# Three one-element clears on GpSimd between the last scatters and the end of the program

## The chip, the cores and the metric

The kernel runs on one core of one Trainium2 chip. The metric is the device time of one execution in microseconds, the median of several runs. The engines are named as in the profile: PE (TensorE matmul), PEld (TensorE weight load), DVE (VectorE), ACT (ScalarE), POOL (GpSimd) and SP (SyncE). A name with a q behind it (POOLq, SPq) is the engine's instruction sequencer, which loads registers, branches, waits on semaphores and drains.

## The reference

Three stages follow one another: windowed attention with a few global keys (2 batches, 8 heads, 768 positions, head size 64), a dense gated feed-forward layer on the 1536 tokens that result, and a mixture of experts in which each token goes to its two best of eight experts. The last stage is the one that matters here:

```python
for e in range(E):
    for k in range(2):
        mask = top2[:, k] == e
        if not mask.any():
            continue
        h = np.maximum(x[mask] @ w1[e], 0.0)
        out[mask] += top2_w[mask, k, None] * (h @ w2[e])
```

The output is 1536 x 512 in float32.

## The kernel before

**The stages.** Attention and the dense layer are interleaved over tiles of 128 tokens. The router then gives every token a slot with each of its two experts, and writes token number and weight to a table in DRAM. The experts run as nine units, numbered 0 to 8. Units 0 and 1 share the expert that leads early, each later unit has one expert of its own with a capacity that falls from 480 to 368 tokens. A unit gathers its tokens' rows, runs two matrix products over eight blocks of the hidden size (`up` at L1041, `down` at L1058 or L1081), and then adds its weighted result to the output.

**How a unit adds to the output.** The output lies in DRAM and is cleared early. For each of its tiles of up to 128 tokens a unit gathers the rows that stand there (`old`, L1018) into a tile `y`, DVE adds the weighted result to `y` (L1110), and `store` writes `y` back by an indirect DMA that POOL issues (L1114). Here an indirect DMA from `y` to the output is called a scatter. Unit 8 is the last. It has 368 slots, so three tiles of 128, 128 and 112 rows, and three scatters. `store` is called for them in the last two lines of `Unit.run`:

```python
            for s, m in self.tiles:
                store(s, m)
```

**What stands behind the scatters.** After the last unit every engine loads a flag (`values_load`, L1302) that says whether an expert had more tokens than its capacity, and branches (L1303) over a slow general path that these inputs don't need. Then the context that builds the program is left (L1382), and it closes the program by itself: SP waits for the semaphore of every DMA and engine, every engine drains and reports to POOL, POOL gives the word to go on, clears a range of semaphores, and there is a second such round. None of that is written in the kernel.

**What sets the order.** Each engine works through its own list of instructions in order. Waits between engines, and between a DMA and an engine, are put in by the framework from what each instruction reads and writes: an instruction that overwrites a tile waits for the semaphore of a DMA that still reads the tile. The scatters' semaphores are called DMASW in the listings of the order.

Of the kernel before, what the change touches and what calls it, by code (L numbers as in the profile page):

```python
# [107 lines left out]
def fused(ctx: ExitStack, tc: tile.TileContext, q, k, v, n_global, n_local, w_gate, w_val, w_out,  # L108
          rms_g, w_router, w_noise, noise, w1, w2, out):
    nc = tc.nc  # L110
# [13 lines left out]
    E, _, F2 = w1.shape  # L124
# [99 lines left out]
    def follow(a, b):  # L224
        tc.add_manual_dep(a, b.name, mybir.DependencyInfo(mybir.DependencyClass.NoSync, mybir.DependencyReason.DATA),
                          reason="order")
# [716 lines left out]
    class Unit:  # L943
# [78 lines left out]
        def run(self, side):  # L1022
            n, cap, gh, gl = self.n, self.cap, self.gh, self.gl
            ending = n == E and len(self.tiles) < 4

            def cuts(s):

                return (slice(0, DM // 2), slice(DM // 2, DM)) if ending and s + 1 == len(self.tiles) else (slice(0, DM),)
# [72 lines left out]
            down(FB2 - 1, prev)  # L1101
            mf = self.me.bitcast(F32)
            done = []

            def store(s, m, turned=None):
                if n > 1:
                    y = self.ys.pop(s)
                    for x, cols in enumerate(cuts(s)):
                        got = acc[s + x][:m, cols] if turned is None else turned[:m, cols]
                        nc.vector.scalar_tensor_tensor(y[:m, cols], got, mf[:m, s, 1:2], y[:m, cols], op0=ALU.mult, op1=ALU.add)  # L1110
                else:
                    y = sb.tile([P, DM], F32, name=f"y{n}_{s}", tag="acc", bufs=NACC)
                    nc.vector.tensor_scalar(y[:m], acc[s][:m], mf[:m, s, 1:2], None, op0=ALU.mult)
                st = nc.gpsimd.indirect_dma_start(  # L1114
                    out=out, out_offset=bass.IndirectOffsetOnAxis(ap=self.me[:m, s, 0:1], axis=0), in_=y[:m],
                    in_offset=None, bounds_check=NT - 1, oob_is_err=False)
                for o in done:
                    tc.declare_no_dep(st.ins, o, reason="a token has one slot per expert")
                done.append(st.ins)
            if wide:  # L1120
                nt = len(self.tiles)
                hs = [pools["b"].tile([P, 2, 2, DC, P], U16, name=f"oT{n}_{x}", tag="raw", bufs=NRAW["b"]) for x in range(2)]
                e, m = self.tiles[-1]
                if m < P:
                    nc.gpsimd.memset(hs[e // 2][:, e % 2].rearrange("p t c q -> p (t c) q")[:, :, m:], 0)
                for c in range(DC):
                    for x in range(2):
                        w = min(2 * P, cap - 2 * x * P)
                        src = acc[c][:, 2 * x * P:2 * x * P + w].bitcast(U16)
                        if w % P and w > P:  # L1130
                            pieces = [(0, 1, P), (1, 1, w - P)]
                        else:
                            pieces = [(0, -(-w // P), min(w, P))]
                        for s0, k, q in pieces:
                            o = hs[x][:, s0:s0 + k, :, c, :q].rearrange("p s t q -> p t s q")
                            i = src[:, 2 * s0 * P:2 * s0 * P + 2 * k * q].rearrange("p (s q t) -> p t s q", t=2, q=q)
                            if c % 2:
                                nc.vector.tensor_copy(o, i)
                            else:
                                nc.scalar.activation(o, i, AF.Copy)  # L1140

                def back(s, m, words, act):
                    pt = sb.tile([P, 512], F32, name=f"pb{n}_{s}", tag="wc", bufs=2)
                    cp = nc.scalar.activation(pt[:m].bitcast(U16).rearrange("p (c q t) -> p t c q", t=2, c=DC),
                                              words[:m].rearrange("p (t c) q -> p t c q", t=2), AF.Copy)
                    follow(cp.ins, act)
                    store(s, m, pt)
                for s, m in self.tiles:
                    if s % 2 == 0:
                        words = sb.tile([P, 2, 2 * DC, P], U16, name=f"ob{n}_{s}", tag="words", bufs=2)  # L1150
                    nc.sync.dma_start_transpose(words[:, s % 2], hs[s // 2][:, s % 2].rearrange("p t c q -> p (t c q)"))
                    tail.append(partial(back, s, m, words[:, s % 2]))
                return
            for s, m in self.tiles:
                store(s, m)

    units = [Unit(0, 0, 0, 0, EARLY), Unit(1, 0, 0, EARLY // P, CAP - EARLY)]

# [3 lines left out]
    n = 0  # L1162
# [224 lines left out]
```

## Time and profile before

| what | us |
|---|---|
| median of 3 runs | 763.89 |
| lowest and highest run | 762.65 and 764.69 |
| the profiled execution, its time | 762.32 |
| the profiled execution, span from first to last instruction | 760.5 |
| PE busy in it | 735.9 |
| POOL busy in it | 318.8 |

The profiled execution's span is 1.8 us shorter than its time; this lies around the program and holds nothing of the kernel. Its time is 1.6 us below the median of the three runs, and these three lie within 2.0 us. PE works for 97% of the span, and the rest of the span is mostly its two ends.

### The profile page before, as it was taken

Reading aid. Unit: us, or ns where it says so; the run is one execution under the profiler, and the core shown is the slowest. Engines: PE = TensorE matmul, PEld = TensorE weight load, DVE = VectorE, ACT = ScalarE, POOL = GpSimd, SP = SyncE. Lnnn points to the kernel's source line nnn. Section 1 sums busy time; section 2 is a strip of 40 time slices with the busy share of each in tenths; the row PEclk is TensorE's granted clock in tenths of the full one; section 3 lists DMA queues with packets and bytes.
Section 4 is the critical chain, followed back from the end, with each engine's and each line's share of the span. In section 5 each row is a group of like instructions: output and inputs, shape, how many; then the busy total and the mean of one; then the engine's idle time right before and its main releaser. Section 6 shows DMA issues by size and latency. Waiting matters only on the chain.

```text
span 760.5 us, 13550 instructions
## 1 busy us (share of the span) xinstructions
PE 735.9 (97%) x4763; PEld 666.6 (88%) x4763; DVE 485.8 (64%) x1134; ACT 410.2 (54%) x878; POOL 318.8 (42%) x350
## 2 busy tenths in 40 slices
PE   9999989999999999999999999999999999999993
PEld 6788989889988888889999989888999999999993
DVE  5998899885497888334535568844555646665641
ACT  5777778675454443114332456536676757776630
POOL 3348853421476566001543144562234345353411
PEclk9999999999999999999999999999999999999997
DMA  8454457533243840002234511989396979898611
GB/s 199 126 166 126 119 135 152 97 85 70 89 135 111 250 137 1 1 6 106 56 57 91 188 29 49 310 240 281 88 264 186 281 175 285 206 323 169 212 41 37
DMA packets 183159, 107.98 MB, mean 142 GB/s; under 512 B 114193, under 2 KB 165393, under 8 KB 183088
## 3 DMA queue, kind: packets, MB, share of 16 engines
q1 hardware_dynamic: 174240, 84.61, 43.0%
q0 software_dynamic: 7120, 19.32, 7.8%
q10 hardware_dynamic: 1728, 3.15, 1.3%
q8 instruction: 39, 0.64, 0.4%
q14 instruction: 32, 0.26, 0.1%
HBM read 75.23 MB, written 16.49 MB: 121 GB/s over the span
## 4 chain that ended last, share of the span: by engine, by line
PE 79%; DVE 7%; DMA 5%; issue 4%; ACT 2%; POOL 1%; SPq 0%; POOLq 0%; ACTq 0%; DVEq 0%
PE pz L1041 17%; PE pz L705 14%; PE acc L732 12%; PE ac L1081 11%; PE pg L705 5%; PE pv L705 5%; PE ac L1058 5%; PE ps L432 3%; PE po L500 1%; DMA ph<-h 1%; PE lg L816 1%; DMA rv<-in_moe_w_val_dram 1%; PE pt L384 1%; PE po L496 1%; DMA y<-out_dram,ic 1%
## 5 line engine op out<-in xcount | busy, mean ns | idle before, releaser
L1041 PE MATMUL pz<-gh,sa 128*128 128x256 f32 (+7 forms) x576 | 154.0, 335 | 2.0 <-POOL sa L686 1.3
L1041 PEld LDWEIGHTS pz<-gh,sa 128*128 128x128 f32 x576 | 103.6, 188 | 7.3 <-POOL sa L686 1.8
L1041 PE MATMUL pz<-gl,sa 128*128 128x256 f32 (+7 forms) x288 | 96.4, 335 | 0.0
L732 PE MATMUL acc<-wo,dh 128*128 128x512 f32 x288 | 88.8, 399 | 0.7 <-ACT dh L718 0.5
L1081 PE MATMUL ac<-zh,sb 128*128 128x480 f32 (+4 forms) x320 | 84.7, 357 | 0.0
L1048 ACT ACTIVATE zh<-pz 128x256 fp32r<-128x256 f32 (+7 forms) x72 | 35.2, 488 | 80.5 <-PE pz L1041 80.5
L1049 DVE SCALAR_TENSOR_TENSOR zl<-pz,zh 128x256 fp32r<-128x256 f32 (+7 forms) x72 | 39.7, 552 | 58.3 <-ACT zh L1048 58.0
L705 PE MATMUL pz<-xTh,wg 128*128 128x256 f32 x352 | 73.9, 286 | 1.3 <-ACT wg L653 1.3
L705 PE MATMUL pz<-xTh,wv 128*128 128x256 f32 x352 | 73.6, 287 | 0.0
L1114 POOL DMA_INDIRECT out_dram<-y,me x30 | 34.2, 1141 | 72.6 <-DVE y L1110 68.7
L1081 PEld LDWEIGHTS ac<-zh,sb 128*128 128x128 f32 x320 | 59.6, 188 | 3.2
L705 PEld LDWEIGHTS pz<-xTh,wg 128*128 128x128 f32 x352 | 58.3, 190 | 3.8 <-ACT wg L653 1.5
L719 POOL TENSOR_TENSOR dl<-u,dh 128x256 fp32r<-128x256 f32 (+1 forms) x38 | 36.9, 972 | 56.6 <-ACT dh L718 31.9
L686 DVE TENSOR_TENSOR sb<-wab,sb 128x512 fp32r<-128x512 f32 x67 | 47.4, 707 | 19.7 <-ACT sb L682 16.8
L686 DVE TENSOR_TENSOR sa<-wab,sa 128x512 fp32r<-128x512 f32 x60 | 44.6, 745 | 23.6 <-ACT sa L682 23.1
L682 ACT ACTIVATE sa<-wab 128x512 fp32r<-128x512 f32 x72 | 44.9, 625 | 27.4 <-PE ac L1081 14.0
L732 PEld LDWEIGHTS acc<-wo,dh 128*128 128x128 f32 x288 | 51.2, 189 | 9.3 <-ACT dh L718 0.7
L705 PEld LDWEIGHTS pz<-xTh,wv 128*128 128x128 f32 x352 | 57.9, 190 | 0.3
L1041 PEld LDWEIGHTS pz<-gl,sa 128*128 128x128 f32 x288 | 54.1, 188 | 2.6 <-DVE gl L1013 0.3
L732 PE MATMUL acc<-wo,dl 128*128 128x512 f32 x144 | 53.5, 397 | 0.0
L1081 PE MATMUL ac<-zl,sb 128*128 128x480 f32 (+4 forms) x160 | 52.4, 358 | 0.0
L1058 PE MATMUL ac<-sb,zh 128*128 128x512 f32 (+1 forms) x176 | 50.6, 375 | 0.0
(255 smaller groups left out, 1841.8 us busy)
## 6 DMA issues: line engine op xcount, KB each, us to landing
wab<-in_moe_w_dram SPq DMA_DIRECT2D x128, 256.0 KB, 6.3
rg<-in_moe_w_gate_dram SPq DMA_DIRECT2D x12, 512.0 KB, 4.5
rv<-in_moe_w_val_dram SPq DMA_DIRECT2D x12, 512.0 KB, 3.6
ro<-in_moe_w_out_dram SPq DMA_DIRECT2D x12, 512.0 KB, 3.6
vn<-in_v_dram SPq DMA_DIRECT2D x12, 256.0 KB, 3.8
out_dram<-zero SPq DMA_DIRECT2D x1, 3072.0 KB, 14.0
x2d<-x ACTq DMA_DIRECT2D x12, 256.0 KB, 5.0
x2p<-hw SPq DMA_DIRECT2D x12, 256.0 KB, 4.6
```

What stands on the lines that cost most here:

```text
L432: seq(nc.tensor.matmul(o, qT[a, h], kT[c][sl, h // 2, C0:], start=(n == 0), stop=(n == len(prods) - 1)))
L682: cp = nc.scalar.activation(wp[:, 0], src, AF.Copy)
L686: sub = (nc.gpsimd if pool else nc.vector).tensor_sub(wp[:, 1], src, wp[:, 0].bitcast(F32))
L705: mm = nc.tensor.matmul(pz, a[:, cs], x[:, tt:tt + nt, c, :], start=(n == 0), stop=(n == 3 * DC - 1))
L719: (nc.gpsimd if ci < len(CHUNKS) - 1 else nc.vector).tensor_sub(dl, u, dh.bitcast(F32))
L732: nc.tensor.matmul(acc[t], a[:, tt], w, start=(f == CHUNKS[ci][0] and n == 0), stop=(end and n == 2))
L1041: mm = nc.tensor.matmul(pz[:, :cap], a[:, cs], x[:, c, :cap], start=(k == 0), stop=(k == 3 * DC - 1))
L1048: self.act = nc.scalar.activation(dh[:, :cap], pz[:, :cap], AF.Relu).ins
L1049: nc.vector.scalar_tensor_tensor(dl[:, :cap], pz[:, :cap], 0.0, dh[:, :cap].bitcast(F32), op0=ALU.max, op1=ALU.subtract)
L1058: mm = nc.tensor.matmul(o, a[:, s * P:s * P + m], w[:, cuts(s)[x]], start=(f == 0 and k == 0), stop=(f == FB2 - 1 and k == 2)).ins
L1081: nc.tensor.matmul(acc[c][:, :cap], w[:, c * P:(c + 1) * P], a[:, :cap], start=(f == 0 and k == 0), stop=(f == FB2 - 1 and k == 2))
L1114: st = nc.gpsimd.indirect_dma_start(out=out, out_offset=bass.IndirectOffsetOnAxis(ap=self.me[:m, s, 0:1], axis=0), in_=y[:m], in_offset=No ...
```

## The change

`Unit.run` keeps the `y` tiles that it stores. In unit 8 (n == E, and E is 8) POOL overwrites the first element of each of the three tiles with zero, after the three scatters have been issued. Each tile is still being read by its scatter, so each clear waits for the semaphore of its scatter. Nothing reads the tiles afterwards, and the output is not touched.

```diff
             down(FB2 - 1, prev)
             mf = self.me.bitcast(F32)
             done = []
+            sent = []
...
                 done.append(st.ins)
+                sent.append(y)
...
             for s, m in self.tiles:
                 store(s, m)
+            if n == E:
+                for y in sent:
+                    nc.gpsimd.memset(y[:1, :1], 0.0)
```

The instructions move at one place, the end of POOL's list. This is that place before: the three gathers of the old rows, the three scatters (`out_dram<-y`), the load of the flag and the branch. DMASW0 to DMASW7 are semaphores of POOL's DMAs, and `DVE` in brackets is a wait for VectorE.

```order
L1018 DMA y_0_8791<-out_dram,ic_8313 128x512 [waits DMASW7_49,DMASW6_49,DMASW5_49]
L1018 DMA y_1_8828<-out_dram,ic_8313 128x512
L1018 DMA y_2_8865<-out_dram,ic_8313 112x512
L1114 DMA out_dram<-y_0_8791,me_8184 1536x512 [waits DMASW1_49,DMASW2_49,DMASW0_49,DVE_49]
L1114 DMA out_dram<-y_1_8828,me_8184 1536x512 [waits DVE_49]
L1114 DMA out_dram<-y_2_8865,me_8184 1536x512 [waits DVE_49]
L1302 TENSOR_LOAD flag [waits DVE_49]
L1303 COMPARE_AND_BRANCH
```

And this is the same place with the change (lines are later by one to five).

```order
L1115 DMA out_dram<-y_0_8791,me_8184 1536x512 [waits DMASW1_49,DMASW2_49,DMASW0_49,DVE_49]
L1115 DMA out_dram<-y_1_8828,me_8184 1536x512 [waits DVE_49]
L1115 DMA out_dram<-y_2_8865,me_8184 1536x512 [waits DVE_49]
L1160 MEMSET y_0_8791 1x1 [waits DMASW3_49]
L1160 MEMSET y_1_8828 1x1 [waits DMASW4_49]
L1160 MEMSET y_2_8865 1x1 [waits DMASW5_49]
L1307 TENSOR_LOAD flag [waits DVE_49]
L1308 COMPARE_AND_BRANCH
```

Three clears stand between the last scatter and the load of the flag, each with a wait for one scatter's semaphore. Nothing moved ahead of them, and the other engines' lists are the same but for line numbers.

## Rows read from the trace of the kernel before

**Rows 1.** Busy time of each engine by stretch, at the end of the program.
```profile
core 0: us, PE busy (x) PEld busy (x) DVE busy (x) ACT busy (x) POOL busy (x), PEclk, DMA share, GB/s
700.00:720.00 20.00, 20.00 (x103) 18.13 (x102) 11.25 (x19) 12.49 (x21) 7.85 (x9) 1.00 0.73 235
740.00:749.00 9.00, 8.00 (x47) 7.04 (x46) 4.80 (x8) 1.92 (x4) 1.72 (x2) 1.00 0.06 23
749.00:751.00 2.00, 0.00 (x0) 0.00 (x0) 0.00 (x0) 0.00 (x0) 1.25 (x2) 1.00 0.47 172
751.00:753.00 2.00, 0.00 (x0) 0.00 (x0) 0.00 (x0) 0.00 (x0) 0.00 (x0) 0.55 0.25 78
753.00:755.00 2.00, 0.00 (x0) 0.00 (x0) 0.00 (x0) 0.00 (x0) 0.00 (x0) 0.50 0.00 0
755.00:760.00 5.00, 0.00 (x0) 0.00 (x0) 0.00 (x0) 0.00 (x0) 0.00 (x0) 0.50 0.00 0
```

**Rows 2.** The chain that ended last, its last four pieces: start us, us, what.
```profile
748.29 1.00 POOL out_dram L1114
749.29 0.08 issue
749.37 0.05 POOLq L1303
749.42 0.13 issue
749.55 1.00 POOLq L1382
```

**Rows 3.** POOL's sequencer in the closing lines: ns min/median/max, first and last start us.
```profile
L1382 POOLq EVENT_SEMAPHORE  x4: 17/17/17, 759.7 to 760.4; - x4
L1382 POOLq DRAIN  x3: 46/113/10069, 749.6 to 760.2; - x3
```

**Rows 4.** The other engines' sequencers in the closing lines, 749 to 760 us.
```profile
L1382 DVEq DRAIN  x2: 10/14/17, 749.0 to 759.9; - x2
L1382 PEldq DRAIN  x2: 8/8/8, 749.2 to 760.0; - x2
```

**Rows 5.** The same for ACT, over the whole span.
```profile
L1382 ACTq DRAIN  x2: 8/8/8, 745.0 to 759.9; - x2
```

**Rows 6.** The same for SP alone, 749 to 754 us.
```profile
L1382 SPq EVENT_SEMAPHORE  x12: 27/28/28, 752.5 to 753.7; - x12
L1382 SPq DRAIN  x2: 7/10/13, 753.8 to 753.8; - x2
```

**Rows 7.** SP's waits from 745 us on: us in total, times, longest.
```profile
SPq L1382 <- PEq L1382: 6.5, 2, 6.0
```

**Rows 8.** POOL's instructions in time at the end: start us, us.
```profile
746.97 1.01 POOL L1114 DMA_INDIRECT out_dram<-y,me  x1 [20.28 <-DVE y L1110]
748.29 1.00 POOL L1114 DMA_INDIRECT out_dram<-y,me  x1 [0.30 <-issue]
749.59 0.96 POOL L1114 DMA_INDIRECT out_dram<-y,me  x1 [0.30 <-issue]
```

**Rows 9.** The last scatter alone (line L1114, from 749.5 us): us to landing.
```profile
DMA to landing us min/median/max: 3.5/3.5/3.5
```

**Rows 10.** Line L1114 from 746 us on, POOL's sequencer ahead of the scatters.
```profile
L1114 POOLq MOVE  x2: 29/29/29, 746.7 to 747.4; - x2
```

**Rows 11.** Line L1110 from 745 us on, DVE's sums that the scatters wait for.
```profile
L1110 DVE SCALAR_TENSOR_TENSOR y<-ac,me,y x4: 484/618/752, 745.9 to 748.0; 128x512 f32<-128x512 f32 x2, 112x256 f32<-112x256 f32 x2
```

**Rows 12.** The load of the flag, line L1302, by engine.
```profile
L1302 SPq TENSOR_LOAD <-flag x1: 268/268/268, 488.4 to 488.4; - x1
...
L1302 POOLq TENSOR_LOAD <-flag x1: 723/723/723, 748.6 to 748.6; - x1
```

**Rows 13.** The smallest clears that POOL makes, line L286.
```profile
L286 POOL MEMSET capv<- x7: 91/91/91, 2.9 to 3.1; 128x1 f32 x7
```

**Rows 14.** POOL's drain at the program's start, line L1368.
```profile
L1368 POOLq DRAIN  x1: 173/173/173, 0.4 to 0.4; - x1
```

**Rows 15.** POOL at an earlier scatter and the instruction behind it.
```profile
718.80 0.97 POOL L1114 DMA_INDIRECT out_dram<-y,me  x1 [0.30 <-DVE zl L1049]
719.79 1.31 POOL L686 TENSOR_TENSOR sa<-wab,sa 128x512 fp32r<-128x512 f32 x1
```

**Rows 16.** All DMAs that POOL issues, by line: count, us to landing.
```profile
out_dram<-y,me POOLq DMA_INDIRECT x30, 4.3
y<-out_dram,ic POOLq DMA_INDIRECT x26, 6.6
...
metad<-meta,si POOLq DMA_INDIRECT x24, 6.5
xg<-x2p,ic POOLq DMA_INDIRECT x22, 5.5
...
xg<-x2d,ic POOLq DMA_INDIRECT x8, 6.6
```

## The prediction, made before the changed kernel ran

> **What bounds the kernel now.** I read the busy times by stretch first, then the end of the chain, then the closing lines engine by engine. The first view shows that PE is the bound almost to the end: it is busy for all of 700 to 720 us, and for 8.00 of the 9.00 us up to 749 us. From 749 us on no matrix, vector or scalar instruction runs, and yet the span goes on to 760.5 us; from 753 us on the DMA engines move nothing either (share 0.00, 0 GB/s) [rows 1]. The change touches only these last 11 us, so only they need to be understood.
>
> The chain ends on POOL: a scatter, the branch, and then a closing instruction that begins at 749.55 us [rows 2]. The chain prints a length of 1.00 us for it; the rows of that line give the true one. It is a DRAIN of 10,069 ns [rows 3], so it ends at 749.55 + 10.07 = 759.62 us, and 0.9 us remain to the end of the span. All others are there long before: the drains of ACT, DVE and PE begin at 745.0, 749.0 and 749.2 us [rows 4, 5], SP passes its twelve waits from 752.5 to 753.7 us and its drain at 753.8 us [rows 6], and then waits 6.0 us [rows 7] (the view names PE's sequencer as the one waited for, but that one was done at 749.2 us, so it is POOL). **POOL's drain alone sets the end**, and it outlasts SP by 5.8 us.
>
> What does the drain wait for? The last scatter is issued from 749.59 to 750.55 us [rows 8] and lands 3.5 us after its start [rows 9], at 753.1 us. SP's waits, which include it, let go at that time, so the landing is real. The drain goes on for 6.5 us more, with nothing in flight and no engine at work. So it does not simply wait for landings. Whether those 6.5 us are work that any first drain has to do, or a price of having begun while scatters were in flight, is the question on which the sign hangs.
>
> **The change, part by part.** The three clears are the nearest to the 128x1 clears of 91 ns [rows 13]; together below 0.3 us, and the first two run while the third still waits. Their waits are the change. Queued behind them on POOL are the load of the flag, the branch, the drain and POOL's word to the closing round, for which all four other engines wait.
>
> Does a clear that waits hold up POOL's sequencer, or does the sequencer go on and drain early? DVE's four sums start from 745.9 to 748.0 us, 750 ns each for the first two [rows 11], so two end at 746.7 and 747.4 us. POOL's sequencer steps from one scatter to the next at 746.7 and 747.4 us [rows 10]: one step when each sum is done. It is held by the wait of the instruction ahead of it. I take that for the clears too.
>
> Then the working is this. The third clear is let go at 753.1 us. The flag's load began at 748.6 us, took 0.72 us [rows 12], and the drain began at 749.55 us [rows 2], so 0.95 us from load to drain. With some 0.05 us for the step, the drain begins at 753.1 + 0.05 + 0.95 = 754.1 us, **4.55 us later** than now.
>
> How long is it then? Two bounds from the same row. All 10.07 us move with it: the span ends 4.6 us later. Or the first 1.00 us of it, up to 750.55 us, was only the wait for the third scatter to be issued [rows 8], which is over by then: 9.07 us remain, it ends at 754.1 + 9.07 = 763.2 us, and the span ends 763.2 - 759.6 = 3.6, say 3.5 us later. I take 3.5, because the overlap with the issue stands in the rows. A cheaper load of the flag (SP's took 0.27 us, not 0.72 [rows 12]) takes off 0.45: 3.1. If the sequencer is not held by the clears, the drain still has to see the third clear done, at about 753.2 us, and then takes its 9.07 us: 762.3 us, 2.6 later. So the likeliest case is +3.5 us between +2.6 and +4.6.
>
> The Trainium skill (Perfetto Trace Analysis, Sequencer-only Instruction) says that the profile's window for a drain begins when its semaphores are satisfied and shows execution alone. By that all 10.07 us would be execution, and the sum +4.6; by the row of the scatter that runs inside the window it is +3.5. No run shown here tells the two apart.
>
> Why is work that moves likelier than a price that goes away? First, the 6.5 us in which nothing is left to wait for. Second, POOL's own instructions are not held by scatters in flight: at 719.79 us a vector operation starts 0.02 us after a scatter's issue ended [rows 15], though scatters take 4.3 us to land [rows 16]. Third, a size that would fit: POOL issued 30 + 26 + 24 + 22 + 8 = 110 DMAs in the program [rows 16], and 9.07 us over 110 is 82 ns each. A drain that goes through all DMAs since the last drain would look like this, and nearly all of these had landed long before. That is an estimate from one division, not a thing seen. POOL's other drains, of 173 ns at the start [rows 14] and 113 and 46 ns at the end [rows 3], have no DMA between them and the drain before, and fit both readings.
>
> Sum: profiled execution 762.32 + 3.5 = 765.8 us. That execution lies 1.6 us under the median of the runs, so against the median it is 763.89 + 3.5 = 767.4 us. Nothing else of the program moves.
>
> **The rivals.** *Faster: the long drain is the price of starting with scatters in flight.* Then a drain that begins at 754.1 us costs what POOL's others do, 0.05 to 0.17 us, POOL gives the word at 754.2 us, just behind SP at 753.8, and the span ends at 754.2 + 0.9 = 755.1 us: 5.4 us less, 758.5 against the median. For it: the only long drain is the only one with DMAs in flight. Against it: the 6.5 us without anything in flight. It decides from the point where the drain after the change lasts under 10.07 - 4.55 = 5.5 us. Chance 0.14. The Trainium skill (VectorE: DVE Perf Modes, The DRAIN you can't avoid) has a rule for it: drains of a program's beginning and end are about 12 ns on all five engines, which would put the end at 755.0 us, 5.5 less. The trace agrees on four engines (7 to 17 ns) and not on POOL.
>
> *No change: the drain's end hangs on something fixed earlier*, such as 9.07 us after the last scatter's issue, however late the drain begins. Since 754.1 us is still ahead of 759.62, all of the new wait would then lie under the old one: 763.9 us. For it: the row can't tell a duration from a deadline. Against: POOL shows no instruction in those 9 us [rows 1]. This is also the case in which the clears do not do what they are for. Chance 0.08.
>
> *The likeliest, later by 2.6 to 4.6 us*: 763.89 + 3.5 = 767.4, and with the runs' own spread 765.2 to 769.3. Chance 0.78.
>
> **How the numbers follow.** A measurement of this kernel can tell about 0.3% from no change, 2.3 us. The likeliest case lies beyond that with all of its bounds, by little at +2.6; I put 0.02 of it within. Faster 0.14, same 0.08 + 0.02 = 0.10, slower 0.76. The range leaves out the faster case and the outer edges; it begins at the low end of the runs of before (762.6, no change) and ends at the highest run plus 4.6 and a little, 769.6.
>
> **What would show it.** In the new profile POOL has three clears, the last at about 753.1 us. If I am right POOL's first closing drain begins near 754.1 us and lasts 9.1 to 10.1 us, and the span is 764 to 765 us. A drain below 0.2 us and a span of 755 us show the faster rival. A drain that ends at 759.6 us shows the deadline. A drain that begins at 749.6 us as before shows that the clears hold nothing. The prediction is wrong in its cause if the drain's length after the last landing depends on what was in flight when it began.

## The result, and the profile after

| | median us | lowest to highest | runs |
|---|---|---|---|
| before | 766.51 | 760.23 to 769.46 | 16 |
| with the three clears | 770.26 | 766.15 to 773.97 | 16 |

The ratio is 1.0051 with a 95% interval of 1.0026 to 1.0076: the change makes the kernel slower by 0.5%, some 3.9 us. The direction and the size against before are as predicted (+3.5 us, 0.46%). The predicted time was not: 770.26 us lies above the range's upper end of 769.6, because before itself came out at 766.51 us over 16 runs, 2.6 us above the three runs that the prediction started from. Those three are the first of the 16.

POOL's closing lines answer to [rows 3]: count, then ns min/median/max, then first and last start in us.

```profile
L1387 POOLq EVENT_SEMAPHORE  x4: 17/17/17, 765.0 to 765.7; - x4
L1387 POOLq DRAIN  x3: 46/107/9057, 755.9 to 765.5; - x3
```

The first closing drain begins at 755.9 us and lasts 9,057 ns. Before, it lasted 10,069 ns, of which the first 1.0 us ran beside the issue of the last scatter; 9.07 us were left then, and 9.06 us it is now, with everything landed before it began (the third clear, which waits for the last landing, runs at 755.11 us, as the next rows show). The drain was not shortened by the wait. It was only started later.

POOL's instructions in time, which answer to [rows 8]: start us, us, and what the engine waited for.

```profile
748.25 1.01 POOL L1115 DMA_INDIRECT out_dram<-y,me  x1 [20.28 <-DVE y L1111]
749.57 1.00 POOL L1115 DMA_INDIRECT out_dram<-y,me  x1 [0.30 <-issue]
750.88 0.96 POOL L1115 DMA_INDIRECT out_dram<-y,me  x1 [0.30 <-issue]
751.80 0.09 POOL L1160 MEMSET y<- 1x1 f32 x1
754.57 0.09 POOL L1160 MEMSET y<- 1x1 f32 x1 [2.69 <-DMA out_dram<-y,me]
755.11 0.09 POOL L1160 MEMSET y<- 1x1 f32 x1 [0.45 <-DMA out_dram<-y,me]
```

The first clear costs no wait, since its scatter has landed by the time the third has been issued. The second and third wait for their scatters, and the third runs at 755.11 us, 4.2 us after its scatter's start. The load of the flag stands behind it, as answers to [rows 12]:

```profile
L1307 POOLq TENSOR_LOAD <-flag x1: 510/510/510, 755.1 to 755.1; - x1
```

Before, it began at 748.6 us, ahead of the last scatter [rows 12]. Now it begins when the third clear is let go, so the waiting clear does hold POOL's sequencer, as [rows 10, 11] had suggested.

The stretches, which answer to [rows 1] (busy us and instructions of each engine, granted clock, DMA share, GB/s):

```profile
752.00:755.00 3.00, 0.00 (x0) 0.00 (x0) 0.00 (x0) 0.00 (x0) 0.09 (x1) 0.63 0.19 57
755.00:757.00 2.00, 0.00 (x0) 0.00 (x0) 0.00 (x0) 0.00 (x0) 0.09 (x1) 0.50 0.00 0
757.00:765.00 8.00, 0.00 (x0) 0.00 (x0) 0.00 (x0) 0.00 (x0) 0.00 (x0) 0.50 0.00 0
```

From 757 to 765 us no engine runs and nothing moves; only POOL's sequencer is in its drain. SP has passed its own waits by 755.9 us and now waits 9.2 us for POOL (its view of waits again names PE's sequencer), where it waited 6.0 us before [rows 7]:

```profile
L1387 SPq DRAIN  x2: 7/10/13, 755.9 to 755.9; - x2
...
SPq L1387 <- PEq L1387: 9.7, 2, 9.2
```

### The profile page after: what moved, and what is told of

It is laid out like the page before. It is cut to its first block, busy times and chain, and to the rows that moved or that the text cites. A ratio compares the mean times of both kernels' runs of the same rounds, so it can differ in the third digit from the quotient of the medians.

```text
span 765.8 us, 13553 instructions
## 1 busy us (share of the span) xinstructions
PE 734.6 (96%) x4763; PEld 665.3 (87%) x4763; DVE 486.5 (64%) x1134; ACT 409.6 (53%) x878; POOL 319.5 (42%) x353
## 4 chain that ended last, share of the span: by engine, by line
PE 76%; DVE 6%; DMA 5%; issue 5%; ACT 4%; POOL 1%; SPq 1%; another core or an unknown queue 1%; POOLq 0%; ACTq 0%; DVEq 0%
PE pz L1041 16%; PE pz L705 14%; PE acc L732 12%; PE ac L1081 10%; PE pg L705 5%; PE pv L705 5%; PE ac L1058 5%; PE ps L432 3%; DMA ph<-h 1%; PE po L500 1%; DMA wab<-in_moe_w_dram 1%; PE lg L816 1%; PE pt L384 1%; PE po L496 1%; DMA out_dram<-y,me 1%
## 5 line engine op out<-in xcount | busy, mean ns | idle before, releaser
L686 DVE TENSOR_TENSOR sb<-wab,sb 128x512 fp32r<-128x512 f32 x67 | 47.6, 711 | 21.7 <-ACT sb L682 16.4
L686 DVE TENSOR_TENSOR sa<-wab,sa 128x512 fp32r<-128x512 f32 x60 | 45.1, 753 | 23.3 <-ACT sa L682 16.8
```

The source lines that it names most:

```text
L686: sub = (nc.gpsimd if pool else nc.vector).tensor_sub(wp[:, 1], src, wp[:, 0].bitcast(F32))
```

## The experiments

**How they are compared.** The start of the last scatter moves from one profiled execution to the next even where the kernels do not differ ahead of it: 749.59 us before [rows 8], 750.88 us with the three clears, 748.58 and 749.36 us with one. In the kernels below that do differ ahead of it, it lies between 745.39 and 753.56 us. So the table at the end of this section takes the time from the last scatter's start to the end of the span. A ratio is to runs of the kernel before in the same group as the experiment's. The two kernels with a drain in unit 8 ran 6 times each, the two with one clear 12 times. The three with further DMAs and the one with a drain in unit 5 ran once each, so of these only the trace is read.

**A drain of POOL's own ahead of the scatters.** The question is whether the closing drain's 9.06 us belong to the DMAs that POOL has issued. If so, a drain in the 20 us in which POOL has nothing to do before the last scatters [rows 8] takes them off the end. On top of before, without clears:

```diff
...
                 if n > 1 and 4 <= f < 4 + len(self.tiles):
                     self.old(f - 4)
+                    if n == E and f == 3 + len(self.tiles):
+                        state["drain"] = nc.gpsimd.drain().ins
+                        follow(state["drain"], self.last_old)
...
+                if n == E:
+                    follow(st.ins, state["drain"])
```

`self.last_old` is the last gather of the unit's old rows, kept in a line that is left out here. `follow(a, b)` puts a behind b in the program's order, without a wait.

> The kernel before, without clears, and with a drain of POOL's own between the last gathers of unit 8 and its three scatters, where POOL has nothing to do for 20 us. Theory (a drain goes through all DMAs that POOL issued since its last drain, 82 ns each): this drain takes 107 x 82 ns = 8.8 us, hidden, and the closing drain has three DMAs left, so it ends with the landing of the last scatter; SP's twelve waits then end the program, and the span is 5.8 us shorter than before (0.8% faster). Rival (a drain behind any DMA of POOL's costs 9.06 us, however many there are): the closing drain still ends 9.07 us after the last scatter's issue, no change.

Measured: ratio 0.9911 (0.9876 to 0.9945), 754.64 us median against 761.26. The new drain's row, the last gather and the next scatter, then POOL's closing lines, POOL's last scatter with its time to landing, and SP's closing drains:

```profile
L1099 POOLq DRAIN  x1: 12502/12502/12502, 720.9 to 720.9; - x1
...
723.14 1.45 POOL L1018 DMA_INDIRECT y<-out_dram,ic  x1 [0.30 <-issue]
744.87 1.01 POOL L1117 DMA_INDIRECT out_dram<-y,me  x1 [20.28 <-DVE y L1113]
...
L1387 POOLq DRAIN  x3: 46/113/3877, 747.4 to 752.5; - x3
...
747.49 0.96 POOL L1117 DMA_INDIRECT out_dram<-y,me  x1 [0.30 <-issue]
DMA to landing us min/median/max: 3.7/3.7/3.7
...
L1387 SPq DRAIN  x3: 7/7/13, 751.9 to 752.2; - x3
```

The drain in the middle took 12.5 us, of which the first 3.7 us waited for two more gathers to be issued (the last from 723.14 us for 1.45), so 8.8 us as expected, and nothing waits for it: the next scatter starts at 744.87 us and waits for DVE as before. The closing drain now ends at 747.4 + 3.9 = 751.3 us, just behind the last landing (751.2 us) and before SP's drains at 751.9, and SP's waits for the landings end the program. From the last scatter's start it takes 5.3 us to the end of the span, where it took 10.9: 5.6 us less, as against 5.8 expected. The rival, a fixed price, falls.

**The same drain, with the clears.**

> The same drain, and the three clears too. Theory: the closing drain begins 0.8 to 1.1 us after the last landing and takes 3 x 82 ns, 0.25 to 0.35 us; about 5.2 us faster than before, and 0.6 us slower than with the drain alone. Rival (9.06 us whatever the count): the closing drain takes 9.06 us after the landing, 3.5 us slower than before.

Measured: ratio 0.9908 (0.9874 to 0.9942). POOL's closing lines and its last scatter:

```profile
L1392 POOLq DRAIN  x3: 46/107/294, 749.7 to 750.6; - x3
...
745.39 0.96 POOL L1118 DMA_INDIRECT out_dram<-y,me  x1 [0.30 <-issue]
```

With three DMAs behind the last drain, and all landed, the closing drain takes 294 ns. The end comes 5.4 us after the last scatter's start, against 5.3 without the clears: once the long drain is gone, the clears cost about nothing, and gain nothing. The 0.6 us expected between the two is not there: POOL's drain ends at 750.0 us and SP's at 749.8 us, so with the clears too the end comes little after SP's waits.

**More DMAs, with many rows and with few.** On top of before, 12 gathers of 8 bytes a row behind the last gathers of unit 8, with 128 rows each (P) in one kernel and 16 in the other:

```diff
...
+                    if n == E and f == 3 + len(self.tiles):
+                        ex = sb.tile([P, 12, 2], I32, name="ex")
+                        behind = self.last_old
+                        for j in range(12):
+                            g = nc.gpsimd.indirect_dma_start(
+                                out=ex[:16, j, :], out_offset=None, in_=metad,
+                                in_offset=bass.IndirectOffsetOnAxis(ap=self.ic[:16, 0:1], axis=0)).ins
+                            follow(g, behind)
+                            behind = g
```

> The same with 16 rows to each of the 12 further gathers. If the DMAs are counted: 0.99 us more again, 10.05 us after the last scatter's issue. If their rows are counted (192 more on 12,808): 0.14 us more. Fixed price or bytes: no more.

Measured with 16 rows, POOL's closing lines and its last scatter:

```profile
L1391 POOLq DRAIN  x3: 46/113/10742, 749.7 to 761.0; - x3
...
749.43 0.96 POOL L1123 DMA_INDIRECT out_dram<-y,me  x1 [0.30 <-issue]
```

The drain ends at 749.70 + 10.74 = 760.44 us, 10.05 us after the issue ended at 750.39: 0.98 us more than before, as expected if DMAs are counted, and not the 0.14 us of their rows or nothing, as for their bytes.

> The kernel before with 12 more DMAs on POOL, in its idle time in unit 8: gathers of 128 rows of 8 bytes each into a tile that nothing reads. Theory: the drain goes through 122 DMAs and ends 122 x 82.4 ns = 10.05 us after the last scatter's issue, in place of 9.07 us (0.99 us more). By rows (12,808 rows before, 1,536 more) it would be 1.09 us more, by bytes moved nothing, by a fixed price nothing.

Measured with 128 rows, the same two views, the scatters in full, and the last one's time to landing:

```profile
L1391 POOLq DRAIN  x3: 46/113/2734, 751.6 to 755.2; - x3
...
746.67 1.00 POOL L1123 DMA_INDIRECT out_dram<-y,me  x1 [4.54 <-DVE y L1119]
747.98 1.00 POOL L1123 DMA_INDIRECT out_dram<-y,me  x1 [0.30 <-issue]
750.75 0.98 POOL L1123 DMA_INDIRECT out_dram<-y,me  x1 [1.77 <-issue]
DMA to landing us min/median/max: 3.2/3.2/3.2
```

A miss: the closing drain took 2.73 us and ended at 754.3 us, 0.4 us after the last landing (3.2 us after its start), and not 10.05 us after the issue. The trace shows something else that is new: the third scatter starts 1.77 us after the second's issue, where this gap is 0.30 in every kernel above. That something done there spared the drain its work is a guess at this point. The last experiment asks how much was left for the drain.

**One clear alone.** On top of the changed kernel, `for y in sent[:1]` in one kernel and `for y in sent[-1:]` in the other.

> The change with the first clear alone. Theory (the long drain starts its 9.06 us when POOL's sequencer and the issue of the last scatter let it, so only the wait up to that point costs): the first scatter lands about when the third has been issued, so the drain starts some 0.2 us later than before and the kernel is 0 to 0.3 us slower than before, which is no change. Rival (a wait of POOL's behind its scatters costs by itself, a third of the whole for each clear): 1.2 us slower than before.

Measured: ratio 1.0017 (0.9988 to 1.0046), no change that can be told.

```profile
L1387 POOLq DRAIN  x3: 46/107/9057, 749.8 to 759.4; - x3
...
748.58 0.96 POOL L1115 DMA_INDIRECT out_dram<-y,me  x1 [0.30 <-issue]
749.50 0.09 POOL L1160 MEMSET y<- 1x1 f32 x1
```

> The change with the last clear alone. Theory: the wait for the last landing is all that counts, so 3.5 to 3.9 us slower than before, as with all three. Rival: 1.2 us slower than before.

Measured: ratio 1.0047 (1.0019 to 1.0074), 3.6 us on 761.96.

```profile
L1387 POOLq DRAIN  x3: 46/107/9057, 754.2 to 763.9; - x3
...
749.36 0.96 POOL L1115 DMA_INDIRECT out_dram<-y,me  x1 [0.30 <-issue]
753.49 0.09 POOL L1160 MEMSET y<- 1x1 f32 x1 [3.16 <-DMA out_dram<-y,me]
```

In both the drain takes the same 9,057 ns. It begins 1.2 us after the last scatter's start with the first clear, and 4.9 us after it with the last one. The wait for the last landing is the whole price, and a clear by itself costs nothing that shows.

**A drain earlier, in unit 5.** On top of the changed kernel, the drain of the first experiment with n == 5.

> The changed kernel with a drain of POOL's own in unit 5, behind its last gather: 80 of POOL's 110 DMAs lie ahead of it and 30 behind. Theory: the closing drain takes 30 x 82.4 ns = 2.47 us, and some 0.05 more. If a drain's price were fixed: 9.06 us; if there were a price only for the first: below 0.3 us. The drain in unit 5 takes about 80 x 82.4 ns = 6.6 us, and may delay unit 6's gathers.

```profile
L1099 POOLq DRAIN  x1: 12212/12212/12212, 633.3 to 633.3; - x1
...
635.96 0.90 POOL L1018 DMA_INDIRECT y<-out_dram,ic  x1 [0.30 <-issue]
...
L1392 POOLq DRAIN  x3: 46/107/2501, 758.1 to 761.2; - x3
...
646.00:660.00 14.00, 9.65 (x39) 9.33 (x38) 3.57 (x7) 3.00 (x6) 5.47 (x5) 0.76 0.97 139
...
PE pz L1041 <- POOL sa L686: 4.3, 1, 4.3
```

The stretch from 646 us on in the trace of before:

```profile
646.00:660.00 14.00, 14.00 (x81) 14.00 (x79) 7.18 (x14) 8.93 (x18) 4.82 (x5) 1.00 0.83 213
```

The closing drain takes 2,501 ns for 30 DMAs, as expected. The drain in unit 5 itself is a miss: it ends at 645.5 us, 8.7 us after its last gather's issue (636.86 us), where 6.6 us were expected for 80 DMAs. Less the 0.05 us without any, that is 108 ns for each. The DMA engines were busy throughout (mean share 1.05 from 633 to 646 us, against 0.20 beside the drain in unit 8), but no run shows whether that is the cause. This drain also does harm: POOL is held by it until 645.5 us, and in the 14 us behind it (PE busy 9.65 us) PE stands still for 4.35 us, 4.3 of them in one wait for an operation of POOL's (L686) that stands behind the held gathers. In the trace of before PE is busy for all 14.

**More DMAs, and the clears,** to see how many were left for the drain.

> The changed kernel with 12 more gathers of 128 rows. Without the clears such a kernel ended 0.4 us after the last landing, against the theory's 10.05 us, and its third scatter began 1.5 us late. If that scatter found no room and POOL struck all finished DMAs off its list at once, few are left for the closing drain: below 0.4 us, and the third scatter is late again. If the list still stands and only the scatter's delay hid it: 10.05 us.

```profile
L1396 POOLq DRAIN  x3: 46/107/777, 757.1 to 758.5; - x3
...
753.22 0.98 POOL L1124 DMA_INDIRECT out_dram<-y,me  x1 [1.77 <-issue]
756.04 0.09 POOL L1169 MEMSET y<- 1x1 f32 x1 [0.97 <-DMA out_dram<-y,me]
```

The third scatter is late by the same 1.47 us. The drain takes 777 ns, with all landed before it began; below 400 was expected. By the price below that is the work of nine DMAs, not of 122. So the list does not stand, and the scatter's delay did not merely hide a long drain; that POOL struck finished DMAs off a list at that scatter fits, but is not seen.

| kernel | POOL's DMAs since its last drain | closing drain, ns | last scatter's start to end of span, us |
|---|---|---|---|
| before | 110 | 9,070 behind the last issue | 760.5 - 749.59 = 10.9 |
| the change | 110 | 9,057 | 765.8 - 750.88 = 14.9 |
| first clear alone | 110 | 9,057 | 759.7 - 748.58 = 11.1 |
| last clear alone | 110 | 9,057 | 764.1 - 749.36 = 14.7 |
| 12 more, 16 rows | 122 | 10,050 behind the last issue | 761.3 - 749.43 = 11.9 |
| 12 more, 128 rows | 122 | 2,734, until 0.4 us behind the landing | 755.5 - 750.75 = 4.8 |
| 12 more, 128 rows, clears | 122 | 777 | 758.7 - 753.22 = 5.5 |
| drain in unit 5, clears | 30 | 2,501 | 761.4 - 753.56 = 7.8 |
| drain in unit 8, clears | 3 | 294 | 750.8 - 745.39 = 5.4 |
| drain in unit 8 | 3 | 3,877, until the landing | 752.8 - 747.49 = 5.3 |

(9,057 - 294) / 107 = 81.9 ns for each DMA, and 294 - 3 x 81.9 = 48 ns without any, close to POOL's shortest drain (46; its others with no DMA ahead of them take 107 to 181). By that line 30 DMAs take 2,505 ns (2,501 measured), and 122 take 10,040 (10,050 with 16 rows). The two kernels with 12 more gathers of 128 rows lie far below the line, and the drain inside unit 5 lies above it.

## Why the prediction missed the time and had the cause

**What bounds the end: right.** POOL's first closing drain alone set the end, and still does.

**What the drain is: right, and now shown.** The division in the third reason, 82 ns for each of 110 DMAs, was marked as an estimate. The closing drains behind 3, 30, 110 and 122 DMAs give 81.9 ns for each DMA that POOL issued since its last drain, landed or not; the 12 further ones with 16 rows cost as much each as the others, of up to 128. Two things do not fit: with 12 further gathers of 128 rows most of the price was gone, and the drain inside unit 5 took 108 ns for each. What the drain does with each DMA inside is not visible.

**The faster rival: fallen.** With nothing in flight the drain takes 9,057 ns, far above the 5.5 us from which that rival decided. The rule of the Trainium skill that stood beside it (VectorE: DVE Perf Modes, The DRAIN you can't avoid), about 12 ns on all five engines, is said there of the drains that the runtime puts around a program. The drains in this program's own closing lines are about that short on four engines, and on POOL they take 46 to 9,057 ns. **The deadline: fallen**, since the drain's end moved with its start.

**The sum: mechanism right, one term off.** From the last scatter's start the end came 4.0 us later (14.9 against 10.9) where 3.5 was taken. The landing was 0.7 us later than the row of before (4.2 us against 3.5), the flag's load 0.2 us shorter (0.51 against 0.72), and the drain's 9.07 us measured 9.06. In the other traces the last landing comes 2.8 to 4.1 us after its scatter's start, so this term moves from run to run, and that 3.5 and 3.9 us came out so close is in part luck. The choice of 9.07 over 10.07 was right: the row's 10,069 ns held 1.0 us of waiting for POOL's own scatter. The rule of the Trainium skill (Perfetto Trace Analysis, Sequencer-only Instruction), by which the window shows execution alone, was read as +4.6 us. The windows here hold waiting too, plainest in the drain behind three DMAs, which shows 3,877 ns while a scatter lands and 294 ns when it has landed.

**The time: wrong.** The step that failed is "against the median it is 763.89 + 3.5", and with it the range's upper end, "the highest run plus 4.6 and a little". Three runs of before were taken for the kernel's level, with a spread of 2.0 us. Those three are part of a group of 16 with a median of 766.51 us, in which single runs lie 9 us apart, and two later groups of the same kernel gave 761.26 and 761.96 us. The range held the uncertainty of the change, and too little of the level's. On the level of the 16 runs the same sum is 766.51 + 3.5 = 770.0 us, against 770.26 measured. What moves the level was not asked here: the traces show it ahead of the last scatter, and the cause stays open. The two later groups ran on two different chips, and for the first the record names none, so a difference between chips is one candidate that no run here separates.

## What to carry to other kernels

The long closing drain on GpSimd was not a wait for the last DMA that a wait elsewhere could replace. Compare such a drain's end with the last landing: here what went on after it was work that moved with the drain's start. Where its length is so many ns for each DMA that GpSimd issued, drain once more while GpSimd is idle, ahead of the last few DMAs: that took 0.9% off this kernel, while the same drain in unit 5, where PE came to wait for GpSimd, let PE stand still for 4.35 us. When a change is worth less than the spread between runs, forecast the difference and give the time the width of the level.

## What the hardware showed that was not expected

With 12 further gathers of 128 rows the third scatter was issued 1.47 us late, both times, and the closing drain that could be read behind it had nine DMAs' worth of work left in place of 122 (777 ns). With 12 gathers of 16 rows there was no such delay. So the delay goes with the rows of the gathers (or their bytes) and not with their number. If POOL struck 113 DMAs off a list in those 1.47 us, that is an estimate of 13 ns each, a sixth of the drain's price. A room for rows that was full at that scatter would explain both, but that is argued and not shown: no run varied the number of rows finely enough to show a bound, and none shows why nine were left.
